# Score products of a fused attention and MLP kernel: stacked float32r for blocks 6 to 23, or float32 on half arrays for all 24

## The chip, the cores and the metric

The kernel runs on one core of a Trainium2 chip. The metric is the device time of one execution in microseconds (us). A core has five engines with queues of their own: TensorE (PE; its weight loads are shown as PEld), VectorE (DVE), ScalarE (ACT), GpSimd (POOL) and SyncE (SP), which issues most of the DMAs here. TensorE writes its results into PSUM, of which the kernel uses eight banks of 128 partitions by 512 float32 values.

## The reference

Causal attention over a window of 96 positions plus 8 global positions, with a linear distance penalty per head, and then an MLP with a sigmoid gate of its own. There are 4 batches, 8 heads, 768 positions and heads of 64; the MLP goes from 512 to 2048 and back, over 3072 rows. The weights of the MLP come as float64.

```python
scores = scale * np.matmul(q, k.transpose(0, 1, 3, 2))
rel = pos[:, None] - pos[None, :]
is_global = pos[None, :] < int(n_global)
is_local = (rel >= 0) & (rel < int(n_local))
keep = is_global | is_local
dist = np.where(is_global & ~is_local, float(n_local), np.abs(rel))
scores = scores - slopes[:, None, None] * dist[None, :, :]
scores = np.where(keep, scores, -1000000000.0)
a = np.exp(scores - np.max(scores, axis=-1, keepdims=True))
a = a / (np.sum(a, axis=-1, keepdims=True) + 1e-09)
x = np.matmul(a, v)                   # then heads side by side: 3072 x 512
h = x @ w_in
return (h * (1.0 / (1.0 + np.exp(-h)))) @ w_out
```

## The kernel before

**Tiling.** Attention goes in 24 blocks `i` of 128 queries: 4 batches with 6 blocks `j` each. A block sees at most 232 keys: its own 128, the 96 before them and the 8 global ones. The first block of a batch (0, 6, 12, 18) has only its own 128. The eight heads are four pairs `hp`; the two heads of a pair lie on partitions 0 to 63 and 64 to 127 of the transposed q and k. The unit `u = 4 * i + hp` counts pairs. The MLP works on 12 groups `g` of two blocks (256 rows), in 16 steps `f` of 128 hidden units.

**A block's work**, by lines: q and k are loaded and transposed by TensorE (`turn`, L467). ScalarE copies them out of PSUM (`high`, L537 and L539; or the stacked functions below). GpSimd carries the last 96 and the global keys from the block before (`carry`, L547 and L549). TensorE makes the scores. VectorE adds the penalty and takes the row maximum (`top_of`, L570), ScalarE takes the exponential and its sum (`expo`, L578), VectorE inverts the sum (L585, L589) and multiplies (L594). TensorE transposes the result (`turn_p`, L608), ScalarE copies it out (`move_p`, L622), and TensorE multiplies it with v, all four pairs in one go (`values_of`, L636). ScalarE and VectorE split the outcome into a high and a low float32r part (L654, L657).

**Two forms of the score product.** Blocks 0 to 5 (`I0=6`) use `scores` (L560): float32, for each head a product of 64 rows, into one PSUM bank for each head. Blocks 6 to 23 use `stack_scores` (L532): float32r, 128 rows. Its operands are made by `stack_high` (L504, L506, L508), `stack_low` (L517) and `twin_low` (L523). For each head, one half of the partitions of the key tile (`KH` or `KL`) holds the rounded part of the key and the other its rest. The query tile (`QH` or `QL`) holds its rounded part on both halves, and tile `R` its rest on both. Two products are added in PSUM, so four for a pair; both heads share one bank.

**The MLP.** Each step has twelve products of 256 columns into the hidden layer (L774: high by high, low by high, high by low), tanh (L780), gate (L784), splitting (L788, L792) and six products of 512 columns (L799). The weights are converted from float64 on the chip by VectorE and ScalarE (L384 to L407), 32 pieces.

**The order** is written out beforehand. `Plan` knows operations with an engine, a cost in ns, a rank and the buffers they use; it plays them through and, whenever an engine is free, takes the ready operation with the smallest rank for which there is room. Each engine's queue runs in that order. Attention has small ranks (near `u`) and the MLP large ones (from 1e3), so that MLP products fill TensorE whenever no attention work is ready. `room` counts the PSUM banks by kind: `po` and `h` for the MLP, `s` for scores, `tp` and `tq` for transposes, `av` for values. `hold` says how many are kept for each kind at a stage; at `HU=13` it goes to the next stage. Scores of later units also wait for an MLP step (`plan.after` with `AHEAD`).

Some waits belong to the stacked form. The low half of q waits for the conversion of the last weight (`o_wf`), and the transposes of block 6 wait for the last `move_p` of block 5, since blocks 0 to 5 keep transposed softmax weights in the buffers that the stacked form needs for `KL` and `QL` (`pt_kind`).

Of the kernel before, what the change touches and what calls it, by code (L numbers as in the profile page):

```python
# [10 lines left out]
F32 = mybir.dt.float32  # L11
F32R = mybir.dt.float32r
# [5 lines left out]
ALU = mybir.AluOpType  # L18
# [3 lines left out]
P = 128  # L22
NPREV = 96
NG = 8
WIN = NPREV + NG + P
# [8 lines left out]

    C0=14, CR=1, LW=1, LB=5, QB=3.5, RI=0.1, RN=0, RP=0.2, RM=0, RV=1.2, RQ=0.1, RB=3, LK=-25, LAG=1,

    BP=(4, 3), NX=20, CF=2, AHEAD=5, SB=(4,), LQ=(1, 2), CN=4, I0=6, QS='ACT',
)


# [130 lines left out]
def attn_moe(ctx, tc, q, k, v, n_global, n_local, w_in, w_out, out):  # L171
    nc = tc.nc
    B, H, S, D = q.shape
    NT, DM = out.shape
    DFF = w_in.shape[1]
    NHP = H // 2
# [42 lines left out]
    def bank(b, n=None, c=None):  # L219
        x = banks[b if isinstance(b, int) else b.bank]  # L220
        if n is None:
            return x
        return x[:, :n] if c is None else x[:, :n * c].rearrange("p (n c) -> p n c", n=n)
# [244 lines left out]

    def whole(i):
        return i < PAR["I0"]

    def part(i, x):
        if x not in blk[i]:
            f = whole(i)
            blk[i][x] = sb2.tile(
                [P, NHP, WIN if x[0] == "K" else P], F32 if f else F32R, name=x + "w" * f, tag=x
            )
        return blk[i][x][:, :, C1:] if x[0] == "K" else blk[i][x]  # L480


# [2 lines left out]

    half = [slice(0, D), slice(D, P)]
    K, Q, R = ("KH", "KL"), ("QH", "QL"), ("R0", "R1")  # L490

    def q_low(i, a):
        if "R" not in blk[i]:
            blk[i]["R"] = x = sb3.tile([P, 2, NHP, P], F32R, name="R", tag="big")
            for b in range(2):
                blk[i][R[b]] = x[:, b]
        return blk[i][R[a]]

    def stack_high(i, nm, a, other):
        ps, x = blk[i]["t", nm, 0], part(i, (K if nm == "k" else Q)[a])  # L500
        r = half[a]
        if not other:
            if nm == "q" and a:
                nc.scalar.mul(x[r], ps[r], 2.0)  # L504
            else:
                nc.scalar.copy(x[r], ps[r])  # L506
        elif PAR["QS"] == "ACT":
            nc.scalar.copy(x[half[1 - a]], x[r].bitcast(F32))  # L508
        else:
            eng = nc.gpsimd if PAR["QS"] == "POOL" else nc.vector  # L510
            eng.tensor_copy(x[half[1 - a]], x[r].bitcast(F32))

    def stack_low(i, nm, a):
        ps, x = blk[i]["t", nm, 0], part(i, (K if nm == "k" else Q)[a])
        r = half[a]
        o = x[half[1 - a]] if nm == "k" else q_low(i, a)[r]
        nc.vector.scalar_tensor_tensor(  # L517
            o, ps[r], 2.0 if nm == "q" and a else 1.0, x[r].bitcast(F32), ALU.mult, ALU.subtract
        )

    def twin_low(i, a):
        x = q_low(i, a)
        nc.scalar.copy(x[half[1 - a]], x[half[a]].bitcast(F32))  # L523

    def stack_scores(i, hp, s):
        t = blk[i]
        w0, n = cols(i)
        ps = bank(s[0], 2, WIN)
        t["s", hp] = [ps[:, a] for a in range(2)]
        for a in range(2):  # L530
            for m, x in enumerate((Q[a], R[a])):
                nc.tensor.matmul(ps[:, a, :n], t[x][:, hp], t[K[a]][:, hp, w0:], start=not m, stop=m == 1)  # L532

    def high(i, nm, p0=0, p1=NHP):
        o, x = part(i, nm.upper() + "H")[:, p0:p1], blk[i]["t", nm, p0][:, p0:p1]
# [5 lines left out]
    def carry(i, x, glob):  # L541
        part(i, x)
        new, old = blk[i][x], blk[i - 1][x]
        old = old if whole(i) else old.bitcast(F32)
        if glob:
            g0 = C1 if i % NJ == 1 else NPREV
            nc.gpsimd.tensor_copy(new[:, :, NPREV:C1], old[:, :, g0:g0 + NG])  # L547
        else:
            nc.gpsimd.tensor_copy(new[:, :, :NPREV], old[:, :, WIN - NPREV:])  # L549

    def cols(i):
        return (0 if i % NJ else C1), (WIN if i % NJ else P)

    def scores(i, hp, s):
        t = blk[i]
        w0, n = cols(i)
        t["s", hp] = ps = [bank(x, WIN) for x in s]
        for a in range(2):
            r = slice(a * D, (a + 1) * D)
            nc.tensor.matmul(ps[a][:, :n], t["QH"][r, hp], t["KH"][r, hp, w0:], start=True, stop=True)  # L560

    def top_of(i, hp, a):
        t = blk[i]
# [31 lines left out]


    def pt_kind(i, hp):
        return "pt" if i >= PAR["I0"] else ("pt", "QL", "KL")[(NHP * i + hp) // 2 % 3]

    def turn_p(i, hp, tp):  # L600
        t = blk[i]
# [54 lines left out]
    def x_low(i):  # L656
        nc.vector.tensor_sub(x_part(i, "xl"), blk[i]["av"], x_part(i, "xh").bitcast(F32))  # L657

    kb = [{x: Buf(x) for x in ("KH", "KL", "QH", "QL", "vn", "vp")} | {"R": Buf("big")} for _ in range(B * NJ)]
    xb = [{x: Buf(x) for x in ("xh", "xl")} for _ in range(NGRP)]  # L660
    o_k = [dict() for _ in range(B * NJ)]
    PARTS = ((0, 1), (1, NHP))
    o_x = [[] for _ in range(NGRP)]
    o_s = {}
    before = {}
    for i in range(B * NJ):
# [14 lines left out]
                    ob[nm + "h", p0, p1] = op("ACT", 51 + 107 * n, rank, (lambda nm=nm, a=p0, b=p1: high(0, nm, a, b)), [o], [tp, hi])  # L681
        for nm in "kq" if i else "":
            xn, tp = Buf(in_kind(i, nm)), Buf("tq")
            hi, lo = kk[nm.upper() + "H"], kk[nm.upper() + "L"]
            o = op("DMA", 1456, rank - lr, (lambda i=i, nm=nm: load(i, nm)), (), [xn], PAR["DL"])
            if i == PAR["I0"]:
                before["lent"] = before["move"]
            o = op("PE", 440, rank, (lambda i=i, nm=nm, tp=tp: turn(i, nm, tp)), [o, before.get("lent")], [xn, tp, hi] if whole(i) else [xn, tp, hi, lo])
            if i >= PAR["I0"]:
                hs = [op("ACT", 500, rank, (lambda i=i, nm=nm, a=a: stack_high(i, nm, a, False)), [o], [tp, x])  # L690
                      for a, x in enumerate((hi, lo))]
                for a, x in enumerate((hi, lo)):
                    y = x if nm == "k" else kk["R"]
                    ob[nm, a] = op("DVE", 718, rank, (lambda i=i, nm=nm, a=a: stack_low(i, nm, a)),
                                   hs + ([o_wf] if nm == "q" else []), [tp, x, y])
                    if nm == "q":
                        ob[nm, a, 2] = op(
                            "ACT", 640, rank + PAR["RQ"], (lambda i=i, a=a: twin_low(i, a)), [ob[nm, a]], [y]
                        )
                        ob[nm, a, 1] = op(  # L700
                            PAR["QS"], dict(ACT=628, POOL=1930, DVE=335)[PAR["QS"]], rank + PAR["RQ"],
                            (lambda i=i, nm=nm, a=a: stack_high(i, nm, a, True)), [hs[a]], [x]
                        )
                continue
            ob[nm + "h"] = op("ACT", 583 if nm == "q" else 470, rank, (lambda i=i, nm=nm: high(i, nm)), [o], [tp, hi])
        if j:
            old = o_k[i - 1]
            stacked = i >= PAR["I0"]
            for x, y in ((("KH", ("k", 0)), ("KL", ("k", 1))) if stacked else (("KH", "kh"),)):
                for gl, cost in ((True, 155), (False, 455)):  # L710
                    ob[x, gl] = op(
                        "POOL", cost, rank, (lambda i=i, x=x, gl=gl: carry(i, x, gl)),
                        [*(old[z] for z in ([(y, *x) for x in PARTS] if i == 1 else (y,))), old.get((x, True)), ob[y]],
                        [kb[i - 1][x], kk[x]],
                    )
        o_v = [op("DMA", 1456, rank - lr + 1, (lambda i=i: load(i, "v")), (), [kk["vn"]], PAR["DL"])]
        if j:
            o_v.append(op("DMA", 750, rank - lr + 1, (lambda i=i: load_prev(i)), before["v"],
# [3 lines left out]
        last, o_m, pts = None, [], []  # L722
        for hp in range(NHP):
            u = NHP * i + hp
            stacked = i >= PAR["I0"]
            s, pe, pt, tp = [Buf("s") for _ in range(1 if stacked else 2)], Buf("pe"), Buf(pt_kind(i, hp)), Buf("tp")
            ks = [kk[x] for x in (("KH", "KL", "QH", "QL") if stacked else ("KH", "QH")) + (("R",) if stacked else ())]
            n = cols(i)[1]
            o = op("PE", 440 if stacked else 736 if j else 560, u,
                   (lambda i=i, hp=hp, s=s, f=stack_scores if stacked else scores: f(i, hp, s)),  # L730
                   [x for y, x in ob.items() if i or y[1] <= hp < y[2]] + [before.get("s")], s + ks)
            before["s"] = o_s[u] = o
            if not u:
                for x in later:
                    plan.after(x, o)
            if u == PAR["HU"]:
                o["hold"] = 1
            o_e = []
            for a in range(2):
                x = op("DVE", 318 if j else 210, u, (lambda i=i, hp=hp, a=a: top_of(i, hp, a)),  # L740
                       [o, o_b[j == 0, hp], before.get("top") if not a else None], [s[a % len(s)], pe])
                if not a:
                    before["top"] = x
                o_e.append(op("ACT", ACT(n, 112) + 186, u, (lambda i=i, hp=hp, a=a: expo(i, hp, a)), [x], [pe]))
# [341 lines left out]
```

## Time and profile before

| | us |
|---|---|
| runs before: median (lowest, highest) of 3 | 715.28 (714.9, 715.79) |
| profiled execution: first to last instruction | 712.7 |
| TensorE busy | 701.2 |
| VectorE busy | 475.1 |
| ScalarE busy | 419.5 |
| GpSimd busy | 25.4 |

The profiled execution lists its instructions with start, duration and line of the source; L560 is line 560 of the kernel above. A matmul's duration includes the time until its result is in PSUM, and matmuls overlap. How long TensorE is taken by one is read from the starts of successive matmuls. A float32 product stands in the trace as two records, a float32r product as one. "128*128" after an operation gives active rows by columns of the array.

### The profile page before, as it was taken

What the parts mean: (1) busy time and instruction counts of PE and PEld (TensorE: products, weight loads), DVE (VectorE), ACT (ScalarE), POOL (GpSimd) and SP (SyncE); (2) the same over time, 40 slices, a digit from 0 to 9 for tenths busy, and PEclk for the clock granted to TensorE, in tenths of its full rate; (3) what the DMA queues carried; (4) which work ended last, traced back from release to release, by engine and by line L of the source; (5) the groups of instructions that cost most, each with busy time, mean ns of one, the idle gap of its engine ahead of it and who ended that gap; (6) DMA issues with size and microseconds to landing.
All of it is one profiled execution on the core that took longest, in us unless ns stands there. A gap on an engine that the chain in (4) does not pass through costs nothing.

```text
span 712.7 us, 13915 instructions
## 1 busy us (share of the span) xinstructions
PE 701.2 (98%) x5108; PEld 626.0 (88%) x5108; DVE 475.1 (67%) x1489; ACT 419.5 (59%) x1092; POOL 25.4 (4%) x83
## 2 busy tenths in 40 slices
PE   8999999999999999999999999999999999999996
PEld 5777999889989999998999998999999999998995
DVE  6999999786666656656666565765665666443332
ACT  6976544696756656657566565565674756443221
POOL 2000000000000000000000000000000000000000
PEclk9999999999999999999999999999999999999998
DMA  9985646341422405224124142231330412000001
GB/s 187 232 264 149 188 123 184 90 133 47 116 74 72 116 3 144 60 57 134 46 72 116 31 116 83 64 102 52 97 93 24 132 31 57 30 1 1 30 0 35
DMA packets 102655, 63.95 MB, mean 90 GB/s; under 512 B 76820, under 2 KB 93460, under 8 KB 102580
## 3 DMA queue, kind: packets, MB, share of 16 engines
q1 hardware_dynamic: 102432, 62.86, 31.9%
q8 instruction: 42, 0.69, 0.4%
q14 instruction: 33, 0.27, 0.1%
q10 hardware_dynamic: 148, 0.13, 0.1%
HBM read 52.43 MB, written 6.29 MB: 82 GB/s over the span
## 4 chain that ended last, share of the span: by engine, by line
PE 93%; DVE 5%; ACT 1%; issue 0%; DVEq 0%
PE bank L774 38%; PE bank L799 38%; PE bank L636 5%; PE bank L608 5%; PE bank L532 4%; PE bank L467 2%; DVE pe L570 1%; DVE pe L594 1%; ACT pe L578 1%; DVE wf L390 0%; PE bank L560 0%; PE bank L910 0%; DVE xl L657 0%; DVE wf L396 0%; DVE wf L384 0%; ACT QHw L537 0%
## 5 line engine op out<-in xcount | busy, mean ns | idle before, releaser
L774 PE MATMUL bank<-xh,WIH 128*128 128x256 f32 x768 | 224.4, 292 | 0.0
L774 PE MATMUL bank<-xl,WIH 128*128 128x256 f32 x768 | 216.2, 282 | 0.1
L774 PE MATMUL bank<-xh,WIL 128*128 128x256 f32 x768 | 215.1, 280 | 0.0
L774 PEld LDWEIGHTS bank<-xh,WIH 128*128 128x128 f32 x768 | 144.6, 188 | 10.7 <-issue 3.4
L774 PEld LDWEIGHTS bank<-xl,WIH 128*128 128x128 f32 x768 | 144.7, 188 | 6.8 <-DVE xl L657 0.3
L774 PEld LDWEIGHTS bank<-xh,WIL 128*128 128x128 f32 x768 | 144.8, 189 | 0.1
L780 ACT ACTIVATE th<-bank 128x256 f32<-128x256 f32 x192 | 73.6, 383 | 105.7 <-PE bank L774 93.6
L799 PE MATMUL bank<-WOH,gh 128*128 128x512 f32 x336 | 135.2, 402 | 0.6 <-ACT gh L788 0.6
L799 PE MATMUL bank<-WOH,gl 128*128 128x512 f32 x336 | 132.5, 394 | 0.0
L799 PE MATMUL bank<-WOL,gh 128*128 128x512 f32 x336 | 132.1, 393 | 0.0
L788 ACT CAST gh<-th 128x256 fp32r<-128x256 f32 x192 | 77.2, 402 | 77.4 <-PE bank L799 57.3
L784 DVE SCALAR_TENSOR_TENSOR th<-th,bank 128x256 f32<-128x256 f32 x192 | 80.0, 417 | 56.9 <-ACT th L780 54.9
L792 DVE TENSOR_TENSOR gl<-th,gh 128x256 fp32r<-128x256 f32 x192 | 81.2, 423 | 52.4 <-ACT gh L788 48.9
L578 ACT ACTIVATE pe<-pe,NM 128x232 f32<-128x232 f32 (+1 forms) x192 | 91.0, 477 | 34.5 <-DVE NM L570 32.6
L570 DVE CUSTOM_DVE_ANT_0 pe<-bank,B 128x232 f32<-128x232 f32 (+1 forms) x192 | 68.5, 374 | 53.0 <-PE bank L532 52.7
L799 PEld LDWEIGHTS bank<-WOH,gl 128*128 128x128 f32 x336 | 63.1, 188 | 15.5 <-DVE gl L792 0.4
L799 PEld LDWEIGHTS bank<-WOH,gh 128*128 128x128 f32 x336 | 63.4, 189 | 7.3 <-ACT gh L788 0.8
L799 PEld LDWEIGHTS bank<-WOL,gh 128*128 128x128 f32 x336 | 63.4, 189 | 6.8
L622 ACT COPY pt<-bank 128x512 f32<-128x512 f32 (+1 forms) x80 | 43.8, 549 | 29.4 <-PE bank L608 29.3
L608 PE MATMUL bank<-ident,pe 128*128 128x128 f32 (+1 forms) x352 | 55.6, 276 | 1.9 <-DVE pe L594 1.6
L594 DVE TENSOR_SCALAR pe<-pe,rs 128x232 f32<-128x232 f32 (+1 forms) x192 | 56.2, 329 | 1.6
L608 PEld LDWEIGHTS bank<-ident,pe 128*128 128x128 f32 (+1 forms) x352 | 41.3, 136 | 12.5 <-DVE pe L594 4.3
(126 smaller groups left out, 863.6 us busy)
## 6 DMA issues: line engine op xcount, KB each, us to landing
c<-in_moe_w_in_dram SPq DMA_DIRECT2D x16, 512.0 KB, 4.6
c<-in_moe_w_out_dram SPq DMA_DIRECT2D x16, 512.0 KB, 3.8
vn<-in_v_dram SPq DMA_DIRECT2D x24, 256.0 KB, 3.6
w<-in_moe_w_in_dram SPq DMA_DIRECT2D x12, 512.0 KB, 3.8
w<-in_moe_w_out_dram SPq DMA_DIRECT2D x12, 512.0 KB, 3.7
kn<-in_k_dram SPq DMA_DIRECT2D x23, 256.0 KB, 4.3
qn<-in_q_dram SPq DMA_DIRECT2D x23, 256.0 KB, 3.1
out_dram<-osb SPq DMA_DIRECT2D x23, 256.0 KB, 2.8
```

Source lines behind the costliest of these rows:

```text
L570: nc.vector.tensor_tensor_reduce(t["p", hp][:, a, :n], t["s", hp][a][:, :n], B1[:, hp] if i % NJ else B0[:, hp], -SC / (1 + a), 3.0e38, AL ...
L578: nc.scalar.activation(x, x, AF.Exp, bias=NM[:, i * H + h:i * H + h + 1], scale=-1.0, accum_out=t["sum", hp][:, a:a + 1],)
L594: nc.vector.tensor_scalar(x, x, t["inv", hp][:, a:a + 1], None, ALU.mult)
L608: nc.tensor.transpose(ps[:n, c, a], pe[:, a, c0:c0 + n], ident)
L622: nc.scalar.copy(t["pt", hp][:, c], t["tp", hp][:, c])
L636: nc.tensor.matmul(pav[r, hp], x[:, 2 * hp + a], pt[:P if c else C1, c, a], start=not c or not i % NJ, stop=c == 1,)
L774: nc.tensor.matmul(ph, w[:, c, fs], x[:, c], start=not c and not n, stop=c == NCC - 1 and n == 2)
L780: nc.scalar.activation(th, mo["ph", g, f], AF.Tanh, scale=0.5)
L784: nc.vector.scalar_tensor_tensor(gf, gf, 1.0, mo["ph", g, f], ALU.add, ALU.mult)
L788: nc.scalar.copy(gh, mo["th", g, f])
L792: nc.vector.tensor_sub(gl, mo["th", g, f], mo["gh", g, f].bitcast(F32))
L799: nc.tensor.matmul(po, a[:, s], w_o(w, f), start=f == 0 and n == 0, stop=f == NFC - 1 and n == 2)
```

## The change

All 24 blocks use float32 products of 64 rows for each head. The stacked form goes, with its five functions, its tile `R`, its waits and the parameters `I0` and `QS`. Two pairs of heads are now one operation of TensorE, four products behind one another (block 0 keeps its first two pairs apart). A run takes two PSUM banks: each holds the scores of the same head of both pairs, 2 x 232 values. The maxima of the second pair wait for the same operation as those of the first. All blocks keep transposed softmax weights in three kinds of buffers in turn. GpSimd carries one tile of keys instead of two, and the planned costs of scores and carries are changed.

```diff
-    BP=(4, 3), NX=20, CF=2, AHEAD=5, SB=(4,), LQ=(1, 2), CN=4, I0=6, QS='ACT',
+    BP=(4, 3), NX=20, CF=2, AHEAD=5, SB=(4,), LQ=(1, 2), CN=4,
...
-    def stack_scores(i, hp, s):
-        t = blk[i]
-        w0, n = cols(i)
-        ps = bank(s[0], 2, WIN)
-        t["s", hp] = [ps[:, a] for a in range(2)]
-        for a in range(2):
-            for m, x in enumerate((Q[a], R[a])):
-                nc.tensor.matmul(ps[:, a, :n], t[x][:, hp], t[K[a]][:, hp, w0:], start=not m, stop=m == 1)
...
-    def scores(i, hp, s):
+    def scores(i, hps, s):
         t = blk[i]
         w0, n = cols(i)
-        t["s", hp] = ps = [bank(x, WIN) for x in s]
-        for a in range(2):
-            r = slice(a * D, (a + 1) * D)
-            nc.tensor.matmul(ps[a][:, :n], t["QH"][r, hp], t["KH"][r, hp, w0:], start=True, stop=True)
+        ps = [bank(x, 2, WIN) for x in s]
+        for m, hp in enumerate(hps):
+            t["s", hp] = [x[:, m] for x in ps]
+            for a in range(2):
+                r = slice(a * D, (a + 1) * D)
+                nc.tensor.matmul(
+                    ps[a][:, m, :n], t["QH"][r, hp], t["KH"][r, hp, w0:], start=True, stop=True
+                )
...
-        return "pt" if i >= PAR["I0"] else ("pt", "QL", "KL")[(NHP * i + hp) // 2 % 3]
+        return ("pt", "QL", "KL")[(NHP * i + hp) // 2 % 3]
...
+    BATCH = ([(0,), (1,), (2, 3)], [(0, 1), (2, 3)])
...
-            if i == PAR["I0"]:
-                before["lent"] = before["move"]
...
-            o = op("PE", 440 if stacked else 736 if j else 560, u,
-                   (lambda i=i, hp=hp, s=s, f=stack_scores if stacked else scores: f(i, hp, s)),
-                   [x for y, x in ob.items() if i or y[1] <= hp < y[2]] + [before.get("s")], s + ks)
-            before["s"] = o_s[u] = o
+            hps = next(x for x in BATCH[i > 0] if hp in x)
+            if hp == hps[0]:
+                s = [Buf("s"), Buf("s")]
+                o = op("PE", 200 + len(hps) * (385 if j else 218), u,
+                       (lambda i=i, hps=hps, s=s: scores(i, hps, s)),
+                       [x for y, x in ob.items() if i or y[1] <= hps[-1] < y[2]] + [before.get("s")],
+                       s + [kk["KH"], kk["QH"]])
+                before["s"] = o_s[u] = o
+            o = before["s"]
...
-            if u == PAR["HU"]:
+            if u == PAR["HU"] - 1:
                 o["hold"] = 1
...
-                       [o, o_b[j == 0, hp], before.get("top") if not a else None], [s[a % len(s)], pe])
+                       [o, o_b[j == 0, hp], before.get("top") if not a else None], [s[a], pe])
```

More of the change, by code (lines that the diff above doesn't have):

```diff
@@ L467, in turn @@
             nc.tensor.transpose(ps[:, hp], blk[i][nm][:, 2 * hp:2 * hp + 2, :], ident)
-    def whole(i):
-        return i < PAR["I0"]
     def part(i, x):
         if x not in blk[i]:
[L476 to L479, printed above, removed]
+            blk[i][x] = sb2.tile([P, NHP, WIN if x[0] == "K" else P], F32, name=x)
         return blk[i][x][:, :, C1:] if x[0] == "K" else blk[i][x]
[L489 to L523, printed above, removed]
-    def stack_scores(i, hp, s):
-        t = blk[i]
-        w0, n = cols(i)
-        ps = bank(s[0], 2, WIN)
-        t["s", hp] = [ps[:, a] for a in range(2)]
-        for a in range(2):
-            for m, x in enumerate((Q[a], R[a])):
-                nc.tensor.matmul(ps[:, a, :n], t[x][:, hp], t[K[a]][:, hp, w0:], start=not m, stop=m == 1)
     def high(i, nm, p0=0, p1=NHP):
@@ L543, in carry @@
         new, old = blk[i][x], blk[i - 1][x]
-        old = old if whole(i) else old.bitcast(F32)
         if glob:
@@ L657, in x_low @@
         nc.vector.tensor_sub(x_part(i, "xl"), blk[i]["av"], x_part(i, "xh").bitcast(F32))
-    kb = [{x: Buf(x) for x in ("KH", "KL", "QH", "QL", "vn", "vp")} | {"R": Buf("big")} for _ in range(B * NJ)]
+    kb = [{x: Buf(x) for x in ("KH", "KL", "QH", "QL", "vn", "vp")} for _ in range(B * NJ)]
     xb = [{x: Buf(x) for x in ("xh", "xl")} for _ in range(NGRP)]
@@ L683, in attn_moe @@
             xn, tp = Buf(in_kind(i, nm)), Buf("tq")
-            hi, lo = kk[nm.upper() + "H"], kk[nm.upper() + "L"]
+            hi = kk[nm.upper() + "H"]
             o = op("DMA", 1456, rank - lr, (lambda i=i, nm=nm: load(i, nm)), (), [xn], PAR["DL"])
-            if i == PAR["I0"]:
-                before["lent"] = before["move"]
[L688 to L704, printed above, removed]
+            o = op("PE", 440, rank, (lambda i=i, nm=nm, tp=tp: turn(i, nm, tp)), [o], [xn, tp, hi])
             ob[nm + "h"] = op("ACT", 583 if nm == "q" else 470, rank, (lambda i=i, nm=nm: high(i, nm)), [o], [tp, hi])
@@ L707, in attn_moe @@
             old = o_k[i - 1]
[L708 to L715, printed above, removed]
+            for gl, cost in ((True, 270), (False, 540)):
+                ob["KH", gl] = op(
+                    "POOL", cost, rank, (lambda i=i, gl=gl: carry(i, "KH", gl)),
+                    [*(old[z] for z in ([("kh", *x) for x in PARTS] if i == 1 else ("kh",))), old.get(("KH", True)), ob["kh"]],
+                    [kb[i - 1]["KH"], kk["KH"]],
+                )
         o_v = [op("DMA", 1456, rank - lr + 1, (lambda i=i: load(i, "v")), (), [kk["vn"]], PAR["DL"])]
@@ L724, in attn_moe @@
             u = NHP * i + hp
-            stacked = i >= PAR["I0"]
-            s, pe, pt, tp = [Buf("s") for _ in range(1 if stacked else 2)], Buf("pe"), Buf(pt_kind(i, hp)), Buf("tp")
-            ks = [kk[x] for x in (("KH", "KL", "QH", "QL") if stacked else ("KH", "QH")) + (("R",) if stacked else ())]
+            pe, pt, tp = Buf("pe"), Buf(pt_kind(i, hp)), Buf("tp")
             n = cols(i)[1]
-            o = op("PE", 440 if stacked else 736 if j else 560, u,
-                   (lambda i=i, hp=hp, s=s, f=stack_scores if stacked else scores: f(i, hp, s)),
-                   [x for y, x in ob.items() if i or y[1] <= hp < y[2]] + [before.get("s")], s + ks)
-            before["s"] = o_s[u] = o
+            hps = next(x for x in BATCH[i > 0] if hp in x)
[7 more added lines that the diff above has]
+            o = before["s"]
             if not u:
```

## The prediction

> **What bounds the kernel now.** I read the page first: span, busy shares, granted clock, then the chain that ended last, by engine and by line.
>
> ```profile
> span 712.7 us, 13915 instructions
> PE 701.2 (98%) x5108; PEld 626.0 (88%) x5108; DVE 475.1 (67%) x1489; ACT 419.5 (59%) x1092; POOL 25.4 (4%) x83
> PEclk9999999999999999999999999999999999999998
> PE 93%; DVE 5%; ACT 1%; issue 0%; DVEq 0%
> PE bank L774 38%; PE bank L799 38%; PE bank L636 5%; PE bank L608 5%; PE bank L532 4%; PE bank L467 2%; DVE pe L570 1%; DVE pe L594 1%; ACT pe L578 1%; DVE wf L390 0%; PE bank L560 0%; PE bank L910 0%; DVE xl L657 0%; DVE wf L396 0%; DVE wf L384 0%; ACT QHw L537 0%
> ```
>
> TensorE holds 93% of the chain, at a granted clock of nine tenths or more in all slices but the last. A busy TensorE can still hide waits, since the ends of matmuls are modelled. So I went on to the chain in order of time (start, length, what) and to busy time by stretch (length, then PE, PEld, DVE, ACT, POOL, each with its count; then the granted clock and the DMA columns).
>
> ```profile
> 45.98 0.61 DVE xl L657
> 46.64 1.93 PE bank L774 x14
> ...
> 159.38 1.42 PE bank L774 x12
> ```
>
> ```profile
> 0.00:46.60 46.60, 41.51 (x345) 30.60 (x345) 40.46 (x190) 37.57 (x115) 5.93 (x23) 1.00 0.92 229
> 46.60:75.00 28.40, 28.34 (x209) 23.68 (x210) 28.40 (x95) 19.31 (x54) 0.00 (x0) 1.00 0.58 172
> 75.00:145.00 70.00, 70.00 (x475) 63.18 (x474) 65.30 (x139) 37.85 (x82) 1.48 (x4) 1.00 0.51 147
> 145.00:600.00 455.00, 455.00 (x3359) 413.18 (x3358) 297.19 (x933) 285.45 (x740) 17.98 (x56) 1.00 0.29 80
> ```
>
> Until 46.6 us the chain lies mostly on VectorE and ScalarE (startup, softmax, weight conversion). From 46.64 on it is TensorE. The twelve MLP products of one step at L774 take 1.42 us, 0.118 each; all 192 steps at that price make 273 us, and 38% of 712.7 is 271. So little or no waiting hides in that stream. From 46.6 us on, whatever is added to TensorE's stream is added to the result. Work on other engines can count before 46.6 us, and perhaps up to 145, where VectorE is still 93 to 100% busy (65.30 of 70.00, 28.40 of 28.40).
>
> **What the score products cost now.** Blocks 6 to 23 use stacked float32r products of 128 rows (L532), four for a pair of heads. Blocks 0 to 5 use float32 products of 64 rows (L560), two for a pair, each in two records. I price both in place, on TensorE's timeline, from start to start (first number): from the matmul ahead to the point behind at which spacing is ordinary again, less the ordinary spacings. First the stacked form, in a block with 232 columns and in one with 128 (the first of each batch).
>
> ```profile
> 155.65 0.28 PE L774 MATMUL bank<-xh,WIL 128*128 128x256 f32 x1
> 155.77 0.28 PE L532 MATMUL bank<-KH,QH 128*128 128x232 f32 x1
> ...
> 156.10 0.28 PE L532 MATMUL bank<-KL,R 128*128 128x232 f32 x1
> 156.21 0.40 PE L799 MATMUL bank<-WOH,gh 128*128 128x512 f32 x1
> ...
> 302.35 0.28 PE L774 MATMUL bank<-xh,WIL 128*128 128x256 f32 x1
> 302.47 0.22 PE L532 MATMUL bank<-KH,QH 128*128 128x128 f32 x1
> ...
> 302.87 0.48 PE L799 MATMUL bank<-WOH,gh 128*128 128x512 f32 x1
> 303.18 0.40 PE L799 MATMUL bank<-WOL,gh 128*128 128x512 f32 x1
> 303.42 0.39 PE L799 MATMUL bank<-WOH,gl 128*128 128x512 f32 x1
> ```
>
> At 232 columns a pair takes 155.77 to 156.21, 0.44 us, and the matmul ahead of it keeps its 0.12: two pairs 0.88. At 128 columns, 302.35 to 303.18 is 0.83, less an ordinary 0.12 and 0.24: 0.47 a pair, of which 0.07 is the late start at 303.18. Two pairs cost 0.80 to 0.95.
>
> Then the float32 form: a run of one pair in place, and three starts from a stretch in which two pairs followed one another (each row begins at its own pair of matmuls, the two heads side by side on the two halves of the rows).
>
> ```profile
> 50.02 0.28 PE L774 MATMUL bank<-xl,WIH 128*128 128x256 f32 x1
> 50.14 0.28 PE L774 MATMUL bank<-xh,WIL 128*128 128x256 f32 x1
> 50.35 0.66 PE L560 MATMUL bank<-KHw,QHw 64*128 64x232 f32 x4
> 50.94 0.38 PE L774 MATMUL bank<-xh,WIH 128*128 128x256 f32 x1
> 51.16 0.28 PE L774 MATMUL bank<-xl,WIH 128*128 128x256 f32 x1
> ```
>
> ```profile
> 10.58 0.56 PE L560 MATMUL bank<-KHw,QHw 64*128 64x232 f32 x4
> ...
> 10.78 0.56 PE L560 MATMUL bank<-KHw,QHw 64*128 64x232 f32 x4
> ...
> 10.97 0.56 PE L560 MATMUL bank<-KHw,QHw 64*128 64x232 f32 x4
> ```
>
> From 50.14 to 51.16 are 1.02 us, in which two ordinary spacings (0.24) would have stood: a run of one pair costs 0.78. It enters 0.09 late (0.21 for 0.12), lasts 0.59 (50.35 to 50.94), and the matmul behind it is followed 0.10 late (0.22 for 0.12). A further step starts every 0.195 (10.58 to 10.97 are two), and a second pair adds two steps, 0.39. A run of two pairs then costs 0.78 + 0.39 = **1.17 us**: four steps of streaming, 0.78, and 0.39 of entry, first weight load and exit, paid once.
>
> For 128 columns no pair stands in place among L774, so I join rows: one run of one pair, and one step of the value products at L636, float32 on half arrays with the same 128 columns.
>
> ```profile
> 5.46 0.49 PE L560 MATMUL bank<-KHw,QHw 64*128 64x128 f32 x4
> 5.88 0.33 PE L467 MATMUL bank<-ident,kn 128*128 128x128 f32 x1
> ...
> 300.37 0.39 PE L636 MATMUL bank<-pt,vn 128*64 128x128 f32 x4
> 300.59 0.39 PE L636 MATMUL bank<-pt,vp 104*64 104x128 f32 x4
> ```
>
> 0.42 for the first pair, 0.22 for two further steps, 0.19 for entry and exit as above: 0.83 for two pairs.
>
> The Trainium skill (TensorEngine Tiling (Array Packing), Key Properties) says that a change of the tiling mode drains TensorE. The row at 50.35 agrees, with 0.09 us lost ahead of the 64-row matmul. By that rule the stacked form, which never leaves the whole array, pays nothing at its borders, and the row at 155.77 shows that too: the rule speaks against this change.
>
> **The change, part by part.**
>
> *Products of blocks 6 to 23.* 15 blocks with 232 columns hold 30 runs: 30 x (1.17 - 0.88) = +8.7 us. Three blocks with 128 columns hold 6: 6 x (0.83 - 0.95) = -0.7, or +0.2 by the lower stacked price. I take -0.7, the price measured in place.
>
> *Products of blocks 0 to 5.* Two runs that become one save an entry and exit, 0.39. Five runs of one pair lie behind 46.6 us in the trace; two or three merges come of them: -1.0. About five merges lie ahead of it, beside the VectorE and ScalarE chain: 0; were that chain not the limit, -2.0.
>
> *Splitting and copying.* What goes away on VectorE is one group, here its busy time from 133 us on; on ScalarE the copies of a low half stand for six of eight such instructions a block. The third row has the stacked products' first and last start.
>
> ```profile
> 133.00:712.70 579.70, 49.56 (x72) 1.00 0.25 69
> L523 ACT CAST R<-R 64x512 fp32r<-64x512 f32 x36 | 22.3, 619 | 1.1 <-DVE R L517 0.3
> L532 PE MATMUL bank<-KH,QH x72: 221/270/375, 143.4 to 636.9; 128*128 128x232 f32 x60, 128*128 128x128 f32 x12
> ```
>
> VectorE loses 49.6 us, ScalarE some 6 x 18 x 0.62 = 67. GpSimd carries one tile of keys a block instead of two. All of it lies under TensorE's stream, which has no gap to give back: 0, and as it is removed nothing can be uncovered. No DMA of data is added or dropped; the tile for the low half of q gives back a staging buffer, which nothing on the chain waits for: 0.
>
> *Waits.* A run now needs two free PSUM banks at once, and both stay taken until four row maxima (L570) are done, where a pair used one bank for two. Behind a waiting run on TensorE's queue stand all MLP products, and behind those the chain itself. The 72 pairs come in 143.4 to 636.9, two every 14 us, and VectorE is busy 297 of 455 us there, so banks should be free in time: 0. The bound is a run waiting out two maxima, under 1 us, for 36 runs; below nothing it can't be. Transposed weights of softmax now rotate through three kinds of buffer in all blocks; each comes round after six pairs: 0 for the same reason.
>
> *Sum.* 8.7 - 0.7 - 1.0 = **+7.0 us**. Against the profiled execution: span 712.7 + 7.0 = 719.7. The median of the runs is 715.28, 2.6 above that span; I leave this part as it is: 722.3.
>
> **The rivals.**
>
> *Borders cost nothing in longer runs (faster).* If in a run of two pairs the weight loads and drains hid under streaming, only the steps would count: 30 x (0.78 - 0.88) and 6 x (0.44 - 0.95), together -6.1, with -1.0 as above: 708.2. It decides if entry, first load and exit come to less than about 0.2 us a run. For it: the second pair's steps do follow at 0.195. Against it: 0.39 was measured at the border of a run, and a longer run has the same borders. The Trainium skill (TensorE: Matmul & The Clock Gate, Part 3) has a rule of this kind: tiles on different row groups overlap, and a pack lasts one matmul and some 4 ns a tile. The steps at 10.58 to 10.97 agree with it, the row at 50.35 shows what it leaves out.
>
> *Borders are shared (about no more than half the loss).* Runs may land next to the value products at L636, which leave the whole array themselves. Each such neighbour saves up to 0.2 us; 18 blocks: -3.6, so 718.7, and 716.7 with the early merges. Against it: between 155 and 156 and at 302 the scheduler put products between MLP products, and it does so whenever their operands are ready first.
>
> *Block 6 comes forward (slower).* Its low half of q waited for the last weight; by the row above its products came at 143.4. Its softmax instructions on VectorE:
>
> ```profile
> L570 DVE CUSTOM_DVE_ANT_0 pe<-bank,B 128x128 f32<-128x128 f32 x32 | 8.3, 285 | 5.9 <-PE bank L532 5.6 <-PE bank L560 0.2
> L594 DVE TENSOR_SCALAR pe<-pe,rs 128x128 f32<-128x128 f32 x32 | 8.0, 290 | 0.3
> L585 DVE TENSOR_SCALAR rs<-sm 128x2 f32<-128x2 f32 x96 | 16.3, 169 | 31.9 <-ACT pe L578 30.7
> ```
>
> Freed of that wait, it can start near 70 us and put its softmax, 8 x 0.285 + 8 x 0.290 + 8 x 0.17 = 6.0 us, in front of weight conversions on a VectorE that has no idle time there. If the MLP then waits for weights, the time is up to 722.3 + 6.0 = 728.3. It decides if VectorE, not TensorE, sets the pace between 66 and 130 us. Against it: TensorE is full there too, and gets block 6's products and transposes to do meanwhile.
>
> That the two pairs would not run together I leave out: one function issues all four products, on operands that are ready before the first.
>
> **How the numbers follow.** Forecast 722.3, chance 0.77. Free borders, 708.2: 0.07. Shared borders, 716.7 to 718.7: 0.08. Block 6 forward, up to 728.3: 0.08. The range 717.0 to 728.0 takes the forecast, most of the shared borders (low end), the late starts of the 128-column blocks, the waits for banks and most of the last rival. About 0.2% (1.4 us) is what a measurement of this kernel tells from no change: faster than that only by free borders, 0.07; within it by the low end of shared borders, 0.05; slower 0.88.
>
> **What would show it.** Right: from about 50 us on, runs of eight records of 64x232, some 0.98 us from first start to the next instruction, the entry 0.21 behind L774 and the spacing behind it 0.1 long; VectorE near 425 us busy; TensorE still without gaps. Wrong: a run's whole price near 0.8 in place (free borders), idle time of TensorE between 66 and 145 us that ends with a weight conversion, or TensorE waiting on L570 ahead of a run (banks).

## The result, and the profile after

The changed kernel took 722.84 us (median of 4 runs, 722.54 to 725.66) against 715.13 before, 7.7 us or 1.1% more. The ratio estimated from all the runs is 1.0116, with a 95% interval of 1.0098 to 1.0134. The forecast was 722.3.

The page of the changed kernel: span, busy times, and the chain that ended last.

```profile
span 720.9 us, 13759 instructions
PE 708.0 (98%) x5110; PEld 620.0 (86%) x5110; DVE 424.8 (59%) x1417; ACT 351.7 (49%) x984; POOL 16.1 (2%) x53
PE 90%; DVE 6%; DMA 1%; issue 1%; ACT 1%; SPq 0%; ACTq 0%
PE bank L735 36%; PE bank L710 35%; PE bank L510 6%; PE bank L588 5%; PE bank L560 5%; PE bank L467 3%; DVE pe L522 1%; DVE pe L546 1%; DVE wf L390 1%; DVE wf L396 1%; DMA c<-in_moe_w_in_dram 1%; DVE wf L384 1%; DMA kn<-in_k_dram 1%; DVE gl L728 1%; DVE th L720 0%
```

L710 is now the hidden layer, L735 the output layer, L510 the scores, L588 the value products and L560 the softmax transposes. VectorE and ScalarE lost 50 and 68 us of work, and the kernel still got slower: TensorE is busy 7 us more and stays at 98%. The cut of 11 and 16% fell on engines that worked beside TensorE's stream, and did not shorten it.

TensorE's timeline around a run of 232 columns and one of 128, as they stand in the stream (start, length, what):

```profile
360.20 0.28 PE L710 MATMUL bank<-xl,WIH 128*128 128x256 f32 x1
360.31 0.28 PE L710 MATMUL bank<-xh,WIL 128*128 128x256 f32 x1
360.52 1.05 PE L510 MATMUL bank<-KH,QH 64*128 64x232 f32 x8
361.51 0.50 PE L735 MATMUL bank<-WOH,gh 128*128 128x512 f32 x1
361.84 0.39 PE L735 MATMUL bank<-WOL,gh 128*128 128x512 f32 x1
...
303.57 0.28 PE L710 MATMUL bank<-xh,WIL 128*128 128x256 f32 x1
303.78 0.71 PE L510 MATMUL bank<-KH,QH 64*128 64x128 f32 x8
304.43 0.51 PE L735 MATMUL bank<-WOH,gh 128*128 128x512 f32 x1
304.77 0.39 PE L735 MATMUL bank<-WOL,gh 128*128 128x512 f32 x1
305.00 0.39 PE L735 MATMUL bank<-WOH,gl 128*128 128x512 f32 x1
```

The run enters 0.09 late (0.21 where 0.12 is ordinary), lasts 0.99 (360.52 to 361.51), and the matmul behind it is followed 0.10 late (0.33 for 0.23): 1.18 us in place, with 1.17 forecast. The one of 128 columns has 0.09 + 0.65 + 0.11 = 0.85, with 0.83 forecast.

Where the time came from is read at the last matmul of each trace, first before, then after:

```profile
706.01 0.39 PE L799 MATMUL bank<-w_last,gl 128*128 128x512 f32 x1
```

```profile
712.85 0.40 PE L735 MATMUL bank<-w_last,gl 128*128 128x512 f32 x1
```

TensorE's stream ends 6.8 us later; the sum of the prediction was 7.0. The span grew by 8.2: the other 1.3 us lie behind the last matmul, from whose start the trace before runs on for 6.7 us and this one for 8.1. Over the ten traces of this case that stretch takes 6.7 to 8.9 us, and 8.0 to 8.1 in the changed kernel and three of its variants. What sets it is open, and the prediction has no term for it. The medians differ by 7.7.

### The profile page after: what moved, and what is told of

Read it like the earlier page. It is cut to its first block, busy times and chain, and to the rows that moved or that the text cites. A ratio compares the mean times of both kernels' runs of the same rounds, so it can differ in the third digit from the quotient of the medians.

```text
span 720.9 us, 13759 instructions
## 1 busy us (share of the span) xinstructions
PE 708.0 (98%) x5110; PEld 620.0 (86%) x5110; DVE 424.8 (59%) x1417; ACT 351.7 (49%) x984; POOL 16.1 (2%) x53
## 4 chain that ended last, share of the span: by engine, by line
PE 90%; DVE 6%; DMA 1%; issue 1%; ACT 1%; SPq 0%; ACTq 0%
PE bank L735 36%; PE bank L710 35%; PE bank L510 6%; PE bank L588 5%; PE bank L560 5%; PE bank L467 3%; DVE pe L522 1%; DVE pe L546 1%; DVE wf L390 1%; DVE wf L396 1%; DMA c<-in_moe_w_in_dram 1%; DVE wf L384 1%; DMA kn<-in_k_dram 1%; DVE gl L728 1%; DVE th L720 0%
## 5 line engine op out<-in xcount | busy, mean ns | idle before, releaser
L710 PE MATMUL bank<-xh,WIH 128*128 128x256 f32 x768 | 223.1, 290 | 0.0
L710 PE MATMUL bank<-xl,WIH 128*128 128x256 f32 x768 | 216.2, 282 | 0.0
L710 PE MATMUL bank<-xh,WIL 128*128 128x256 f32 x768 | 214.8, 280 | 0.3 <-DVE WIL L407 0.3
L710 PEld LDWEIGHTS bank<-xh,WIH 128*128 128x128 f32 x768 | 144.5, 188 | 9.1 <-issue 0.8
L710 PEld LDWEIGHTS bank<-xl,WIH 128*128 128x128 f32 x768 | 144.6, 188 | 7.1
L710 PEld LDWEIGHTS bank<-xh,WIL 128*128 128x128 f32 x768 | 144.9, 189 | 0.5 <-DVE WIL L407 0.5
L735 PE MATMUL bank<-WOH,gh 128*128 128x512 f32 x336 | 140.5, 418 | 0.0
L735 PE MATMUL bank<-WOL,gh 128*128 128x512 f32 x336 | 132.1, 393 | 0.4 <-DVE WOL L407 0.4
L735 PE MATMUL bank<-WOH,gl 128*128 128x512 f32 x336 | 132.4, 394 | 0.0
L735 PEld LDWEIGHTS bank<-WOH,gh 128*128 128x128 f32 x336 | 63.1, 188 | 16.8 <-issue 10.5
L735 PEld LDWEIGHTS bank<-WOH,gl 128*128 128x128 f32 x336 | 63.0, 187 | 15.1
L735 PEld LDWEIGHTS bank<-WOL,gh 128*128 128x128 f32 x336 | 63.3, 188 | 6.6 <-DVE WOL L407 0.7
L522 DVE CUSTOM_DVE_ANT_0 pe<-bank,B 128x232 f32<-128x232 f32 (+1 forms) x192 | 63.7, 377 | 3.2 <-PE bank L510 1.4
L546 DVE TENSOR_SCALAR pe<-pe,rs 128x232 f32<-128x232 f32 (+1 forms) x192 | 57.7, 329 | 2.0
L560 PE MATMUL bank<-ident,pe 128*128 128x128 f32 (+1 forms) x352 | 55.5, 275 | 2.3 <-DVE pe L546 2.3
L560 PEld LDWEIGHTS bank<-ident,pe 128*128 128x128 f32 (+1 forms) x352 | 41.3, 136 | 10.8 <-DVE pe L546 2.7
L510 PE MATMUL bank<-KH,QH 64*128 64x232 f32 (+1 forms) x384 | 48.2, 371 | 0.0
```

The lines of the kernel that those rows point to most:

```text
L510: nc.tensor.matmul(ps[a][:, m, :n], t["QH"][r, hp], t["KH"][r, hp, w0:], start=True, stop=True)
L522: nc.vector.tensor_tensor_reduce(t["p", hp][:, a, :n], t["s", hp][a][:, :n], B1[:, hp] if i % NJ else B0[:, hp], -SC / (1 + a), 3.0e38, AL ...
L546: nc.vector.tensor_scalar(x, x, t["inv", hp][:, a:a + 1], None, ALU.mult)
L560: nc.tensor.transpose(ps[:n, c, a], pe[:, a, c0:c0 + n], ident)
L710: nc.tensor.matmul(ph, w[:, c, fs], x[:, c], start=not c and not n, stop=c == NCC - 1 and n == 2)
L735: nc.tensor.matmul(po, a[:, s], w_o(w, f), start=f == 0 and n == 0, stop=f == NFC - 1 and n == 2)
```

## The experiments

One theory had to be told apart from its rivals. The theory: a run pays 0.39 us for leaving and re-entering the whole array (its borders), whatever its length. The rivals: the borders are free in longer runs; the PSUM banks that a run holds are the cost; block 6, freed of its wait, gets in the way of the weights. All times are medians, beside runs of the kernel before on the same chip.

### One pair a run

```diff
-    BATCH = ([(0,), (1,), (2, 3)], [(0, 1), (2, 3)])
+    BATCH = ([(0,), (1,), (2,), (3,)], [(0,), (1,), (2,), (3,)])
```

> All runs of two pairs are split into runs of one pair: 36 more runs in blocks 6 to 23, and two or three more behind 46.6 us in the early blocks. Border theory (0.39 us of entry, first weight load and exit for each run): 38.5 x 0.39 = +15.0, so 738 us, with each run at 0.59 from first start to the next instruction. Free borders: no change, 723. Banks as the cost (two banks held for four maxima): faster than 723, since each run gives its banks back after two maxima. Block 6 coming forward as the cost: 723.

Measured: 737.65 us, 14.8 above the changed kernel. TensorE's timeline of this kernel:

```profile
300.19 0.28 PE L710 MATMUL bank<-xh,WIL 128*128 128x256 f32 x1
300.39 0.66 PE L510 MATMUL bank<-KH,QH 64*128 64x232 f32 x4
300.99 0.50 PE L735 MATMUL bank<-WOH,gh 128*128 128x512 f32 x1
301.32 0.39 PE L735 MATMUL bank<-WOL,gh 128*128 128x512 f32 x1
```

The same products, with the same borders around half as many of them: 0.20, 0.60, 0.33. Behind 46.6 us the trace has 77 runs instead of 38, so 39 more borders for 14.8 us, 0.38 each. Free borders are out. So are the banks as the cost: these runs give theirs back after two maxima, and the kernel is slower. The changed kernel's own trace agrees: each of its 34 runs from 155 us on starts 0.20 or 0.21 us behind the product ahead of it, so none waits longer for its banks.

One more rival is the type: a run differs from the products around it by float32 as well as by the half array. The transposes of the softmax weights (L560) are float32 on the whole array, and in the changed kernel's trace they stand between the same MLP products:

```profile
308.98 0.28 PE L710 MATMUL bank<-xh,WIL 128*128 128x256 f32 x1
309.09 0.38 PE L560 MATMUL bank<-ident,pe 128*128 128x128 f32 x2
309.23 0.36 PE L710 MATMUL bank<-xh,WIH 128*128 128x256 f32 x1
309.43 0.28 PE L710 MATMUL bank<-xl,WIH 128*128 128x256 f32 x1
```

From 308.98 to 309.43 are 0.45 us, less two ordinary spacings (0.24): 0.21 for two records of 128 columns. Two steps of 128 columns in the prediction's rows take 0.22, so nothing is left for a border. The border comes with the half array, not with float32.

### The two heads apart in the queue

```diff
-        for m, hp in enumerate(hps):
-            t["s", hp] = [x[:, m] for x in ps]
-            for a in range(2):
+        for a in range(2):
+            for m, hp in enumerate(hps):
+                t["s", hp] = [x[:, m] for x in ps]
```

> The same products, but within a run both pairs of the first head go before both pairs of the second, so that neighbours in the queue stand on the same half of the rows. If the two halves work side by side only when they alternate in the queue, a run of 232 columns has seven steps of 0.195 us instead of four (the second head can start only when the first head's last step has started): 30 x 0.585 + 6 x 0.33 + 3 x 0.585 in the early blocks = +21.3, so 744 us. Wholly one after the other, eight steps: about 751. If TensorE brings them together itself: 723. The border theory alone says nothing of this; it needs the four steps of 0.195 to be two heads at a time.

Measured: 722.52 us, no change. The expectation of 744 was wrong. A run in this kernel's timeline:

```profile
359.52 0.28 PE L710 MATMUL bank<-xh,WIL 128*128 128x256 f32 x1
359.73 1.06 PE L510 MATMUL bank<-KH,QH 64*128 64x232 f32 x8
360.72 0.50 PE L735 MATMUL bank<-WOH,gh 128*128 128x512 f32 x1
```

0.99 us, as with alternating heads, although in the compiled order both products of one head now stand ahead of both of the other. So either TensorE starts the second head while the first head's products still stand in the queue, or the heads never went side by side and a step of 0.195 us is simply what two products take. The next experiment separates these.

### All products on one half of the rows

```diff
-                r = slice(a * D, (a + 1) * D)
+                r = slice(0, D)
```

> Leaves out the scores of the second head of each pair: its products are made again from the first head's rows, so that all four products of a run stand on the same 64 rows of the array; their number, size and order are those of the changed kernel. If it is the two halves of the rows that let the heads go side by side (whatever their order in the queue), a run has eight steps instead of four: 30 x 0.78 + 6 x 0.44 + 3 x 0.78 in the early blocks = +28.4, so 751 us, with steps one by one at 0.195. If a step of 0.195 us is what two products take anyway, one after the other: 722.7.

Measured: 753.94 us.

```profile
300.38 0.28 PE L710 MATMUL bank<-xh,WIL 128*128 128x256 f32 x1
300.59 1.83 PE L510 MATMUL bank<-KH,QH 64*128 64x232 f32 x8
302.35 0.50 PE L735 MATMUL bank<-WOH,gh 128*128 128x512 f32 x1
302.68 0.40 PE L735 MATMUL bank<-WOL,gh 128*128 128x512 f32 x1
```

The run lasts 1.76 us (300.59 to 302.35) instead of 0.99: four steps more, 0.77. On different halves the two heads do go side by side, in both orders of the queue that were run. The borders are as they were (0.21 and 0.33). The total is 3 us above the expectation, which counted the early blocks only behind 46.6 us. Their runs are longer ahead of it too: the first run behind 46.6 us starts at 51.31 us in the changed kernel and at 55.23 here, 3.9 us later.

### Block 6 waits for the weights again

```diff
-                       [x for y, x in ob.items() if i or y[1] <= hps[-1] < y[2]] + [before.get("s")],
+                       [x for y, x in ob.items() if i or y[1] <= hps[-1] < y[2]] + [before.get("s")] + ([o_wf] if i == NJ else []),
```

> Block 6's first scores wait again for the conversion of the last weight, as in the kernel before. Border theory: TensorE's stream holds the same work in another order, 722.8 within about 1 us; the one gap of some 0.7 us at 102.6 us, which ends with a weight conversion, may go. Block 6 coming forward as the cost: 3 to 6 us faster than 722.8, 717 to 720.

Measured: 722.45 us (722.21 to 722.72), 0.4 less than the changed kernel and within the spread of its runs. In the changed kernel block 6 does come forward (the run at 70.36 below), and the chain from 74 to 103 us lies mostly on VectorE, ending in a gap of TensorE. First the chain, then the timeline, both of the changed kernel:

```profile
70.36 0.65 PE bank L510 x8
...
73.06 1.18 PE bank L735 x5
74.26 0.41 ACT gh L724
74.67 0.43 ACT pe L530 x2
75.10 0.40 DVE gl L728
75.58 0.33 DVE wf L384
```

```profile
102.44 0.28 PE L710 MATMUL bank<-xh,WIH 128*128 128x256 f32 x1
102.56 0.28 PE L710 MATMUL bank<-xl,WIH 128*128 128x256 f32 x1
103.17 0.38 PE L710 MATMUL bank<-xh,WIL 128*128 128x256 f32 x1 [0.34 <-DVE WIL L407]
```

This is a trap in reading: 29 us of the chain lie mostly on VectorE, yet TensorE had work almost all that time, and the whole price is the gap at 102.56 (0.61 us to the next start where 0.12 is ordinary) and a late start behind it (0.23 for 0.12), 0.6 us together. With block 6 held back, TensorE's busy time from 75 to 145 us is full, first in the changed kernel, then in this one (length, PE, PEld, DVE, ACT, POOL):

```profile
75.00:145.00 70.00, 69.66 (x473) 62.48 (x471) 66.12 (x161) 35.64 (x89) 0.81 (x2) 1.00 0.48 138
```

```profile
75.00:145.00 70.00, 70.00 (x479) 62.87 (x478) 67.88 (x166) 37.28 (x92) 0.67 (x2) 1.00 0.47 142
```

The mechanism was there, at a tenth of the 6 us that were its bound.

### The stacked kernel with only the early runs merged

In the kernel before, `scores` takes `hps` as in the change for blocks 0 to 5; `stack_scores` stays for the others. As in the change, `hold=1` begins one unit earlier. The main lines:

```diff
+            hps = (hp,) if stacked else next(x for x in BATCH[i > 0] if hp in x)
+            if hp == hps[0]:
+                s = [Buf("s") for _ in range(1 if stacked else 2)]
...
+            elif hp == hps[0]:
+                o = op("PE", 200 + len(hps) * (385 if j else 218), u,
+                       (lambda i=i, hps=hps, s=s: scores(i, hps, s)),
...
```

> The kernel before, stacked from block 6 on, with only the runs of two pairs in blocks 1 to 5. Border theory: two or three runs fewer behind 46.6 us, where TensorE sets the end, 0.39 us each: 1.0 us faster than before, 714.1; up to 3.0 if the early merges count too. Free borders: as before, 715.1. If VectorE still sets the pace up to 130 us: as before, 715.1.

Measured: 714.15 us, ratio to before 0.9985 (0.9976 to 0.9994). That is 1.1 us less (0.4 to 1.7 by the interval), where the prediction's sum has -1.0. Its trace has two runs of eight records behind 46.6 us in place of five of four. Merging pays where the runs had borders already.

### Fewer borders still: four pairs a run, runs beside the values, and both

The border theory says how to buy the time back without the stacked form. From block 6 on, all four pairs can go in one run (four banks, or two at 128 columns); and the first run of a block can follow directly on the value products, which leave the whole array themselves. The main edits (in the first and third the planner also keeps no bank for `av`, and in the third none for `tp`, at the stage `hold=1`):

```diff
-    BATCH = ([(0,), (1,), (2, 3)], [(0, 1), (2, 3)])
+    BATCH = ([(0,), (1,), (2, 3)], [(0, 1), (2, 3)], [(0, 1, 2, 3)])
...
-            hps = next(x for x in BATCH[i > 0] if hp in x)
+            hps = next(x for x in BATCH[2 if i >= NJ else i > 0] if hp in x)
...
-                s = [Buf("s"), Buf("s")]
+                s = [Buf("s") for _ in range(4 if len(hps) > 2 and j else 2)]
```

```diff
+                if i > NJ and not hp:
+                    plan.after(before["av"], *ob.values())
+                    plan.after(o, before["av"])
+                    pre[u] = before["av"]
...
+                before["av"] = last
...
-            plan.after(o, o_h[divmod(f, NFC)])
+            plan.after(pre.get(u, o), o_h[divmod(f, NFC)])
```

> From block 6 on, one run of four pairs a block instead of two of two: 18 runs instead of 36 (with 232 columns a run takes four PSUM banks, with 128 columns two). Border theory: 18 x 0.39 = 7.0 us less than 722.8, so 715.8, and a run of sixteen records lasts about 1.77 us from first start to the next instruction. Free borders: no change, 722.8. Banks: four are held until eight row maxima are done, and only one is kept for the hidden layer; if that makes TensorE wait, the gain is smaller or gone, above 719, and idle time of TensorE shows between a maximum and the next run.

> Runs of two pairs as in the changed kernel, but the first run of each block from 7 on goes directly behind the value products of the block before (17 more such neighbours than in the changed kernel). Shared borders: one change of mode instead of two at each, up to 0.2 us, so 17 x 0.19 = 3.2 us less than 722.8: 719.6. If what a border costs is the first weight load and not the change of mode, the run still pays it: 722.8 less at most 1.6, 721 or above. Free borders: 722.8. The later start of a block's scores could cost time at the start or make TensorE wait: above 723.

> Both together: one run of four pairs a block from block 6 on, directly behind the value products of the block before (17 more neighbours). Border theory, gains added: 722.8 - 7.0 - 3.2 = 712.6, below the kernel before at 715.3. If the banks run short, above 715.

Measured: 715.38 us for four pairs (ratio to before 1.0010, 0.9998 to 1.0021), 719.36 beside the values (1.0057, 1.0042 to 1.0073), and 712.87 for both (0.9967, 0.9955 to 0.9979). The first and the third in their timelines:

```profile
356.36 0.28 PE L711 MATMUL bank<-xh,WIL 128*128 128x256 f32 x1
356.57 1.84 PE L511 MATMUL bank<-KH,QH 64*128 64x232 f32 x16
358.34 0.50 PE L736 MATMUL bank<-WOH,gh 128*128 128x512 f32 x1
358.68 0.40 PE L736 MATMUL bank<-WOL,gh 128*128 128x512 f32 x1
```

```profile
356.91 0.39 PE L589 MATMUL bank<-pt,vp 104*64 104x128 f32 x4
357.13 0.39 PE L589 MATMUL bank<-pt,vn 128*64 128x128 f32 x4
357.45 1.84 PE L511 MATMUL bank<-KH,QH 64*128 64x232 f32 x16
359.21 0.51 PE L741 MATMUL bank<-WOH,gh 128*128 128x512 f32 x1
```

A run of sixteen records lasts 1.77 us, as expected, with the same 0.21 and 0.34 around it: eight steps for one border. Beside the values the run still enters late (0.32 from the start of the last four value records, where 0.22 is their ordinary step), but the value products' own way back into the whole array is gone. In the changed kernel it stands in the timeline:

```profile
355.07 0.39 PE L588 MATMUL bank<-pt,vn 128*64 128x128 f32 x4
355.39 0.50 PE L735 MATMUL bank<-WOH,gh 128*128 128x512 f32 x1
355.73 0.39 PE L735 MATMUL bank<-WOL,gh 128*128 128x512 f32 x1
```

There the values' exit costs 0.10 (0.32 for 0.22) and 0.11 (0.34 for 0.23), about 0.2 us in all, and that is what a neighbour saves. The gains nearly add up: against 722.84, 7.5 us for 18 fewer borders, 3.5 for 17 shared ones, and 10.0 for both, where the sum is 11.0. The third is the fastest kernel of the study, 0.33% ahead of the kernel before. Four banks held for eight maxima did not make TensorE wait in a way that shows in these times.

## Why the prediction was right

**The bound.** Right: TensorE's stream set the end, and the prices of its products account for what the stream lost, with no gain left over from the work taken off the other engines.

**The price of a run.** Right, 1.17 forecast and 1.18 measured in place for 232 columns, 0.83 and 0.85 for 128. It could be had before the change since each piece stood in the old trace: a border in the early blocks, the step of 0.195 where two pairs happened to meet.

**Blocks 6 to 23.** +8.7 and -0.7 forecast, with the stacked prices read at one place each. Read wherever a pair or a run stands between MLP products behind 145 us, the medians are 0.45 us for a stacked pair of either width (57 pairs of 232 columns, 10 of 128), and 1.18 and 0.85 for a run (30 and 4). That gives 30 x (1.18 - 0.90) = +8.4 and 6 x (0.85 - 0.90) = -0.3; with -1.1 for the early merges +7.0, where TensorE's stream shows 6.8 and the medians 7.7. So 0.88 for two stacked pairs of 232 columns was a little low (some 0.6 us over 30 of them) and 0.95 for 128 too high (0.3 over 6), and it was luck that these misses work against each other. Beyond the products the traces show the stretch behind the last matmul, 1.3 us longer in the profiled execution. The prediction did not cost it, and its share of the 7.7 between the medians is open.

**Early merges.** -1.0 forecast for what lies behind 46.6 us, -1.1 measured alone.

**Costs set to nothing.** Splitting and copying on VectorE and ScalarE, and the two PSUM banks: borne out, by the sum above, which leaves nothing over for them, and by runs that from 155 us on never wait for banks. No experiment took the copies away by themselves. What I had not costed is the gap of 0.6 us at 102.6 us, which belongs to the rival of block 6.

**The rivals.** Free borders fell with the run of one pair. Shared borders did not come about by themselves: in the trace all 36 runs of blocks 6 to 23 stand between MLP products, as I had argued; made to happen, each was worth 0.2 us, as forecast. Block 6 came forward, at 70 us, and cost up to 0.6 us.

**One theory of mine fell**, in the experiments: that heads must alternate in the queue to go side by side. No term of the prediction rested on it.

## What to carry to other kernels

Price a matmul form in place, from the last ordinary start ahead of it to the first ordinary spacing behind it: here a third of the run's cost stood at its borders, outside the run's own steps. A form that leaves the whole array wins or loses by how many products share one border; count borders first, and put runs together or beside others that leave the array too. When one engine's stream has no gaps, count work taken off the others as nothing: here 50 and 68 us less on VectorE and ScalarE did not show in the time.

## What the runs showed of the hardware

Two float32 products on different halves of the rows go side by side even when they don't follow each other in the queue: the run lasted 0.99 us with heads alternating and with heads apart, and 1.76 us with all products on one half. The Trainium skill (TensorE: Matmul & The Clock Gate, Part 3) says that matmuls start and end strictly in queue order; the run with heads apart does not agree with that, since in strict order it would have needed at least seven steps of 0.195 us where it took four.

A float32 run on 64 rows pays about 0.38 us for its borders, by 39 more of them in one experiment (14.8 us), while float32 transposes on the whole array pay nothing that the timeline shows (0.21 us for two records at 309.09). The Trainium skill (TensorEngine Tiling (Array Packing), Key Properties) says that a change of the tiling mode drains TensorE, and these two prices agree with that.
